# Attention, gated MoE and second MoE on one core: the head reordered, a third point for side work, a pair's last operands split one unit later

## The chip, the cores and the metric

One core of one Trainium2 chip runs the whole program. The metric is device microseconds (us) of one execution; lower is better. Three runs of the kernel before give a median of 1201.41 us (1200.02 to 1201.78).

## The reference

Three stages, everything in float32, with N = 6016 rows and C = 256 channels.

```python
qn = q / (np.linalg.norm(q, axis=1, keepdims=True) + 1e-06)
kn = k / (np.linalg.norm(k, axis=1, keepdims=True) + 1e-06)
s = kn.transpose(0, 2, 1) @ qn / tau               # 256 x 256, over the rows
a = softmax(s)
x = (v @ a).reshape(6016, 256)
...
xn = x / sqrt(mean(x * x, -1) + 1e-06) * rms_g     # gated MoE, d_ff 1536
x = (silu(xn @ w_gate) * (xn @ w_val)) @ w_out
...
h = x @ w_in                                       # second MoE, d_ff 2048
out = (h - np.tanh(h)) @ w_out
```

In the two MoE stages every operand is split into a high and a low part, and every product is made of three matmuls (high·high, low·high, high·low). The weights come as 64-bit words and are put together on the chip. (The first code block is shortened: the softmax stands for four lines.)

## The kernel before

Five engines work under one schedule that the Python program writes out by hand: each engine runs its instructions in the order of the program, so a line that is emitted earlier stands earlier in its engine's queue, and an instruction that waits holds up all behind it on that engine. SP issues nearly all DMAs in the same way. PE is TensorE, DVE VectorE, ACT ScalarE.

**The head.** `attention()` reads q and k in 13 chunks (11 of four 128-row groups, then 2 and 1). For every chunk ACT squares q and k (L463) into `sq`, DVE adds the squares to `acc` (L438), and PE adds the products into S (`score`, L433). The last three chunks (`BEHIND`) leave their products for later. Then PE sums `acc` over partitions into `nrm` (L490), DVE makes the reciprocal norms in a chain of 15 short steps (L501 to L508), PE spreads them (`rq_ps`, L514) between the held-back products, and a loop over the two halves of S does the softmax (L528 to L540). What follows makes x for the first two token blocks (L561), its mean square (L585), its norm (`rsqrt_ops`, `r`, L601) and its split.

**The converter.** Nine weight items (`gv0` to `gv5`, gate and value; `w10` to `w12`, output weights) are converted by the generator `conversion()`: ACT starts the item (`w_start`, L273), DVE shifts it (L277), adds the sign (L280) and the low bits (L284), ACT makes the high part `h`, DVE the low part `l` (L141), and a DMA saves it to DRAM (`gv2s<-gv2y`). The generator yields after each step; `PLAN` gives, for places of the head, how many steps to run there, and `need()` forces an item that a product wants.

**Pair 0.** The first two token blocks (512 and 384 wide) go through 12 `gate_block`s each: gate product, value product, `silu`, multiplication, split, and pushes of output products (`A.push`) into a list of fillers that PE takes `LAG` blocks later. Block 1 runs `SKEW` steps behind block 0. Two calls of `side(a, d)` in every block let the waiting generators (`works`: the converter, the preparation of the next pair's operands `x_work`, the sums of weights) run up to d DVE and a ACT steps; a generator may also wait a number of such calls (`yield 4`). Right behind the head stand `split_a()` and, spread over the first steps, the norm chain of block 1 (`post`).

**Pairs 1 to 5** of the first MoE and **p0 to p5** of the second work on two 512-wide token blocks (448 in p0) in Strassen-like units: seven products per unit (X, T, Y, Z), operands B11, T1, T2, B21, T3, B22, T4 prepared by `operands()` from the pair's four blocks. At a unit's start PE makes X and T, ACT copies them to Y and m5 (L138), PE adds T2's product onto Y, DVE adds Y and m5 to Z (L166). `unit()` calls `hurry()`, which runs the list `urgent`, right behind the two copies. At the end of a pair `finish(x_work)` emits all that is left of the next pair's operands: B21, T3, B22 and T4 may only be split once the last unit of the running pair is under way. The scale of x by its norm (`x_0g<-x_0g,rs`, L769) comes before that; it wants a row that goes by DMA through DRAM (`back<-naryp` L758, then `rs<-back` L763).

## Time and profile before

| | value |
|---|---|
| median of three runs | 1201.41 us |
| the profiled execution | 1201.24 us, its span 1199.3 us |
| mean granted TensorE clock | 0.982 |
| PE busy | 1143.6 us (95%) |
| DVE busy | 826.0 us (69%) |
| ACT busy | 690.9 us (58%) |
| PE on the chain that ended last | 78% of the span (DVE 8%, DMA 6%, ACT 5%) |

The profiled execution took 1.9 us more than its span, which starts with the first instruction recorded. PE is busy nearly all the time, so a gain has to come from a stretch in which PE waits, or runs at the lower of its two clock levels (1.2 GHz, shown as 0.50, and 2.4 GHz, shown as 1.00). The stages follow from the names of the matmuls: the head to 74.83, pair 0 to 188.35, pairs 1 to 5 to 293.85, 401.75, 503.13, 602.99 and 694.69, the six pairs of the second MoE to 773.67, 859.86, 942.24, 1025.08, 1107.46 and the end.

### The profile page before, as it was taken

Reading aid. Unit: us, or ns where it says so; the run is one execution under the profiler, and the core shown is the slowest. Engines: PE = TensorE matmul, PEld = TensorE weight load, DVE = VectorE, ACT = ScalarE, POOL = GpSimd, SP = SyncE. Lnnn points to the kernel's source line nnn. Section 1 sums busy time; section 2 is a strip of 40 time slices with the busy share of each in tenths; the row PEclk is TensorE's granted clock in tenths of the full one; section 3 lists DMA queues with packets and bytes.
Section 4 is the critical chain, followed back from the end, with each engine's and each line's share of the span. In section 5 each row is a group of like instructions: output and inputs, shape, how many; then the busy total and the mean of one; then the engine's idle time right before and its main releaser. Section 6 shows DMA issues by size and latency. Waiting matters only on the chain.

```text
span 1199.3 us, 13912 instructions
## 1 busy us (share of the span) xinstructions
PE 1143.6 (95%) x4980; PEld 931.9 (78%) x4980; DVE 826.0 (69%) x1382; ACT 690.9 (58%) x1207; POOL 0.7 (0%) x6
## 2 busy tenths in 40 slices
PE   9689899998999999999999999899999999999998
PEld 8567597786787777778878888788888788888887
DVE  5677576757657666857777787776776776766664
ACT  5454536554655654564565565665665755756655
POOL 0000000000000000000000000000000000000000
PEclk9798999998999999999999999999999999999999
DMA  9535211211311212031020130010110100100000
GB/s 363 202 110 189 71 53 49 71 34 55 107 43 45 88 62 71 27 106 33 29 93 21 34 104 19 18 58 1 36 36 1 62 10 1 62 1 1 36 1 36
DMA packets 37736, 73.04 MB, mean 61 GB/s; under 512 B 6426, under 2 KB 8218, under 8 KB 37668
## 3 DMA queue, kind: packets, MB, share of 16 engines
q1 hardware_dynamic: 37380, 71.12, 18.0%
q10 hardware_dynamic: 288, 1.05, 0.2%
q8 instruction: 39, 0.64, 0.2%
q14 instruction: 29, 0.24, 0.1%
HBM read 52.45 MB, written 19.70 MB: 60 GB/s over the span
## 4 chain that ended last, share of the span: by engine, by line
PE 78%; DVE 8%; DMA 6%; ACT 5%; issue 2%; SPq 0%; ACTq 0%; DVEq 0%
PE acc L147 32%; PE Yh L147 8%; PE Yg L147 5%; PE Yv L147 5%; PE Xh L147 5%; PE Xv L147 3%; PE Xg L147 3%; PE Zh L147 3%; PE Th L147 2%; PE x L147 2%; DMA k<-k_in 2%; PE g L147 2%; PE v L147 2%; PE Zv L147 2%; PE Tv L147 2%
## 5 line engine op out<-in xcount | busy, mean ns | idle before, releaser
L135 ACT ACTIVATE hc<-wc 128x512 fp32r<-128x512 f32 (+1 forms) x192 | 113.8, 617 | 76.9 <-DVE wc L1188 76.9
L141 DVE TENSOR_TENSOR lc<-wc,hc 128x512 fp32r<-128x512 f32 (+1 forms) x192 | 127.3, 674 | 33.1 <-ACT hc L135 33.1
L135 ACT ACTIVATE uc<-t 128x512 fp32r<-128x512 f32 x120 | 72.1, 627 | 87.5 <-DVE t L844 87.4
L141 DVE TENSOR_TENSOR ulc<-t,uc 128x512 fp32r<-128x512 f32 x120 | 79.7, 685 | 10.1 <-ACT uc L135 7.4
L166 DVE TENSOR_TENSOR Zv<-Yv,m5v 128x512 f32<-128x512 f32 x30 | 21.0, 699 | 77.6 <-ACT x_1g L689 43.8
L166 DVE TENSOR_TENSOR Zh<-Yh,m5h 128x512 f32<-128x512 f32 (+1 forms) x48 | 33.0, 687 | 45.6 <-PE Yh L147 41.5
L1188 DVE TENSOR_TENSOR wc<-Yh,wc 128x512 f32<-128x512 f32 (+1 forms) x48 | 32.7, 680 | 28.5 <-ACT wc L1185 28.5
L1185 ACT ACTIVATE wc<-Xh 128x512 f32<-128x512 f32 (+1 forms) x48 | 28.3, 589 | 38.2 <-PE Xh L147 38.2
L166 DVE TENSOR_TENSOR s<-Yh,m5h 128x512 f32<-128x512 f32 (+1 forms) x48 | 32.6, 679 | 24.5 <-PE Yh L147 24.3
L1185 ACT ACTIVATE wc<-Yh 128x512 f32<-128x512 f32 (+1 forms) x48 | 28.3, 589 | 35.9 <-PE Yh L147 35.9
L166 DVE TENSOR_TENSOR Zg<-Yg,m5g 128x512 f32<-128x512 f32 x30 | 21.0, 699 | 35.1 <-PE Yg L147 32.8
L433 PE MATMUL S<-q,k 128*128 128x256 f32 x188 | 44.1, 398 | 1.0 <-DMA k<-k_in 1.0
L1185 ACT ACTIVATE wc<-s 128x512 f32<-128x512 f32 (+1 forms) x48 | 29.9, 623 | 25.1 <-DVE s L166 25.0
L433 PEld LDWEIGHTS S<-q,k 128*128 128x128 f32 x188 | 37.2, 200 | 7.2 <-DMA k<-k_in 1.3
L1188 DVE TENSOR_TENSOR wc<-s,wc 128x512 f32<-128x512 f32 (+1 forms) x48 | 32.7, 681 | 9.4 <-ACT wc L1185 9.4
L438 DVE TENSOR_TENSOR acc<-acc,sq 128x1024 f32<-128x1024 f32 (+1 forms) x24 | 24.0, 1023 | 18.0 <-ACT sq L463 17.6
L147 PE MATMUL Yh<-T2h,l2s 128*128 128x512 f32 (+1 forms) x96 | 30.5, 399 | 4.9 <-ACT Yh L138 4.2
L847 ACT ACTIVATE t<-Zg 128x512 f32<-128x512 f32 x30 | 17.9, 596 | 28.4 <-PE Zg L147 28.4
L166 DVE TENSOR_TENSOR c<-Yv,m5v 128x512 f32<-128x512 f32 x30 | 20.7, 691 | 18.9 <-PE Yv L147 17.3
L1188 DVE TENSOR_TENSOR wc<-Xh,wc 128x512 f32<-128x512 f32 (+1 forms) x48 | 32.6, 679 | 0.9 <-ACT wc L1185 0.5
L1188 DVE TENSOR_TENSOR wc<-Zh,wc 128x512 f32<-128x512 f32 (+1 forms) x48 | 32.3, 672 | 0.0
L147 PE MATMUL Th<-T1h,l2s 128*128 128x512 f32 (+1 forms) x96 | 29.8, 389 | 2.5 <-ACT l2s L135 1.3
(918 smaller groups left out, 3516.3 us busy)
## 6 DMA issues: line engine op xcount, KB each, us to landing
q<-q_in SPq DMA_DIRECT2D x11, 512.0 KB, 9.5
vraw<-vT_in SPq DMA_DIRECT2D x11, 512.0 KB, 3.9
y<-r SPq DMA_DIRECT2D x22, 256.0 KB, 2.0
y<-y SPq DMA_DIRECT2D x20, 256.0 KB, 3.6
outT<-r SPq DMA_DIRECT2D x20, 256.0 KB, 2.1
...
```

Source lines behind the costliest of these rows:

```text
L135: nc.scalar.activation(out=dst, in_=src, func=AF.Copy, scale=scale)
L141: nc.vector.tensor_sub(out=dst, in0=src, in1=f32(hi))
L147: nc.tensor.matmul(out, a, b, start=start and i == 0, stop=i == 2, skip_group_check=True)
L166: nc.vector.tensor_add(out=o, in0=a, in1=b)
L433: nc.tensor.matmul(S[m][:, :C], kt[:, j, m * P:(m + 1) * P], qt[:, j, :], start=(i == 0 and j == 0), stop=(i == NCH - 1 and j == chunks[i] ...
L438: nc.vector.tensor_add(out=out, in0=a, in1=b)
L847: nc.scalar.activation(out=o, in_=a, func=AF.Silu)
L1185: nc.scalar.activation(out=t[c][:, :n], in_=src, func=AF.Tanh)
L1188: nc.vector.tensor_sub(out=t[c][:, :n], in0=src, in1=t[c][:, :n])
```

## The change

The head is written in a new order. All products of the last three chunks with the first half of S stand ahead of `nrm`, those with the second half right behind it, and `rq_ps` after all of them. The squares go through three buffers in turn. `PLAN` puts fewer conversion steps among the squares: none of gv1 before them all are made. The softmax makes both exponentials first and then both divisions. Block 1's norm chain is emitted ahead of the gate blocks, `split_a` moves into the preparation of pair 1.

Every conversion step is now one of DVE or one of ACT, and a generator runs only steps of one engine in one call of `side`. A gate block has three such calls (a new one between `silu` and the multiplication), the first three steps have a thin table of their own (`EARLY`), block 1 runs two steps behind instead of three, and the output products three blocks behind instead of two.

`finish_late` stops the next pair's preparation before B22 and T4 and leaves these two to `urgent`, so that they are emitted inside the next pair's first unit, behind the copies of X and T. It is used at the ends of pairs 1 to 5 and of p0 to p4: ten times; pair 0 keeps `finish`.

```diff
 PLAN = {
-    ("s", 5): 1, ("s", 6): 1, ("s", 7): 1, ("s", 8): 1, ("s", 9): 1, ("c", 0): 1, ("c", 1): 1,
-    ("c", 2): 1, ("c", 3): 1, ("c", 4): 1, ("c", 6): 1,
+    ("s", 4): 1, ("s", 5): 1, ("s", 6): 1, ("s", 7): 1, ("s", 12): 2, ("c", 1): 3, ("c", 2): 1,
+    ("c", 3): 2, ("f", 0): 1, ("f", 1): 0,
 }
-SIDES = (((1, 1), (1, 2)), ((1, 1), (1, 2)))
+EARLY = (((0, 1), (0, 0), (0, 0)), ((0, 1), (0, 0), (0, 0)), ((1, 1), (0, 1), (0, 0)))
+SIDES = (((1, 2), (1, 2), (1, 1)), ((1, 2), (1, 2), (1, 1)))
...
     def can(self, kind):
-        return self.kind == kind and (kind == "A" or self.acted < Work.clock)
+        return self.kind == kind and self.last[kind] < Work.clock
     def run(self):
-        if self.kind == "A":
-            self.acted = Work.clock
+        if self.kind in self.last:
+            self.last["A" if self.kind == "D" else "D"] = Work.clock
...
     def hurry():
-        for op in urgent:
-            op()
-        urgent.clear()
+        while urgent:
+            urgent.pop(0)()
...
         for i, c in enumerate(items):
             y = c["y"].bitcast(I32)
+            yield "D"
             shift(y)
             yield "D"
-            if before:
-                w_low(before)
-                yield "D"
             sign(y, c["raw"][:, :, 1])
+            yield "D"
+            bits(y, c["raw"][:, :, 0])
+            if "saved" in c:
+                nc.sync.dma_start(out=c["saved"], in_=c["y"])
...
+            yield "A"
+            hi_of(c["h"], c["y"])
+            if i + 2 < len(items):
+                w_load(items[i + 2])
             if i + 1 < len(items):
+                yield "A"
                 w_start(items[i + 1])
             yield "D"
...
+            lo_of(c["l"], c["y"], c["h"])
+            c["ready"] = True
...
-                    pool, tag = ((sp, "sq"), (act, "wraw"))[s]
+                    pool, tag = ((sp, "sq"), (act, "wraw"), (act, "vl"))[(2 * i + s) % 3]
...
+            rest = [(i, j) for i in range(NCH - BEHIND, NCH) for j in range(chunks[i][1])]
+            for i, j in rest:
+                score(i, j, 0)
             for s in range(2):
                 for m in range(KC):
...
-            rest = [(i, j) for i in range(NCH - BEHIND, NCH) for j in range(chunks[i][1])]
             for i, j in rest:
-                score(i, j, 0)
+                score(i, j, 1)
...
+        out["late"] = True
         yield from split(("B22", b22), ("T4", t2))
...
+        if p == 1:
+            yield from split_a()
...
+    for op in p1["rs"]:
+        op()
     at("c", 6)
-    split_a()
...
-    SKEW = 3
-    POST = [6, 5, 9]
-    LAG = 2
+    SKEW = 2
+    LAG = 3
...
         silu(t[:, :n], g[:, :n])
+        side(*sides[2])
         mul(t[:, :n], t[:, :n], v[:, :n])
...
+    def finish_late(w, x):
+        while "late" not in x:
+            w.run()
+            hurry()
+        urgent.append(lambda: finish(w))
...
-        finish(x_work)
+        finish_late(x_work, x_next)
```

How the order moves, at the three places that matter. In names, `sq_0` and `sq_1` are squares of q and k, `gv0y` a weight item at work, `gv0h` its high part.

**The head, ACT**, before: the second half of the squares begins.

```order
L273 ACTIVATE gv0y<-gv0raw 128x1024
L463 ACTIVATE sq_0_255<-q_139 128x1024
L463 ACTIVATE sq_1_258<-k_141 128x1024
L273 ACTIVATE gv1y<-gv1raw 128x1024
L463 ACTIVATE sq_0_276<-q_191 128x1024
L463 ACTIVATE sq_1_279<-k_193 128x1024
L135 ACTIVATE gv0h<-gv0y 128x1024
```

And with the change, at the end of the squares:

```order
L460 ACTIVATE sq_0_330<-q_250 128x1024
L460 ACTIVATE sq_1_335<-k_252 128x1024
L460 ACTIVATE sq_0_340<-q_269 128x512
L460 ACTIVATE sq_1_344<-k_271 128x512
L460 ACTIVATE sq_0_348<-q_288 128x256
L460 ACTIVATE sq_1_351<-k_290 128x256
L138 ACTIVATE gv0h<-gv0y 128x1024
L275 ACTIVATE gv1y<-gv1raw 128x1024
L515 ACTIVATE rq<-rq_ps 128x256
```

The start of gv1, which stood between the squares of two chunks, now stands behind all of them, as does the high part of gv0.

**The head, PE**, from `nrm` to the end of S, before:

```order
L490 MATMUL nrm<-ones,acc 128x2 x4
L433 MATMUL S_109<-q_248,k_250 128x256 x4
L433 MATMUL S_109<-q_269,k_271 128x256 x2
L433 MATMUL S_109<-q_290,k_292 128x256
L433 MATMUL S_110<-q_248,k_250 128x256
L514 MATMUL rq_ps<-ident,r__378 128x128 x2
L433 MATMUL S_110<-q_248,k_250 128x256 x3
L433 MATMUL S_110<-q_269,k_271 128x256 x2
L433 MATMUL S_110<-q_290,k_292 128x256
```

With the change:

```order
L430 MATMUL S_109<-q_250,k_252 128x256 x4
L430 MATMUL S_109<-q_269,k_271 128x256 x2
L430 MATMUL S_109<-q_288,k_290 128x256
L490 MATMUL nrm<-ones,acc 128x2 x4
L430 MATMUL S_110<-q_250,k_252 128x256 x4
L430 MATMUL S_110<-q_269,k_271 128x256 x2
L430 MATMUL S_110<-q_288,k_290 128x256
L511 MATMUL rq_ps<-ident,r__380 128x128 x2
```

The first seven held-back products (S_109 is the first half of S) moved ahead of `nrm`, the other seven between `nrm` and `rq_ps`.

**The end of pair 1, DVE**, where pair 2's operands are made (`x_0g` and `x_1g` are x, `rs` its norm, `t_5` unit 5's tiles), before:

```order
L844 TENSOR_TENSOR t_5_2203<-t_5_2203,Yv_2221 128x512
L844 TENSOR_TENSOR t_5_2174<-t_5_2174,c_5_2247 128x512
L141 TENSOR_TENSOR ulc_2265<-t_5_2203,uc_2262 128x512
L769 TENSOR_TENSOR x_0g<-x_0g,rs_0_2192 128x512
L769 TENSOR_TENSOR x_1g<-x_1g,rs_0_2192 128x512
L769 TENSOR_TENSOR x_0g<-x_0g,rs_1_2194 128x512
L769 TENSOR_TENSOR x_1g<-x_1g,rs_1_2194 128x512
L629 TENSOR_TENSOR t_2274<-x_0g 128x512
L141 TENSOR_TENSOR B11l<-x_0g,B11h 128x512
L629 TENSOR_TENSOR t_2280<-x_1g,t_2274 128x512
```

With the change:

```order
L771 TENSOR_TENSOR x_0g<-x_0g,rs_0_2071 128x512
L169 TENSOR_TENSOR t_5_2189<-Yg_2157,m5g_2159 128x512
L771 TENSOR_TENSOR x_1g<-x_1g,rs_0_2071 128x512
L771 TENSOR_TENSOR x_0g<-x_0g,rs_1_2073 128x512
L771 TENSOR_TENSOR x_1g<-x_1g,rs_1_2073 128x512
L628 TENSOR_TENSOR t_2200<-x_0g 128x512
L279 TENSOR_SCALAR y_2118<-y_2118 128x512
L282 SCALAR_TENSOR_TENSOR y_2118<-raw_2087,y_2118 128x512
L144 TENSOR_TENSOR B11l<-x_0g,B11h 128x512
L628 TENSOR_TENSOR t_2231<-x_1g,t_2200 128x512
L169 TENSOR_TENSOR Zv_2239<-Yv_2225,m5v_2227 128x512
L846 TENSOR_TENSOR t_5_2180<-t_5_2180,Xv_2217 128x512
```

The four products with `rs`, which stood behind everything of unit 5, now stand ahead of its value half (`Zv`, `t_5_2180`), and B11's low part with them.

**The end of p1, ACT** (`hc` is a high part of p1's last unit, `Yh` and `m5h` the copies of the first unit of p2), before:

```order
L135 ACTIVATE hc_7195<-wc_7192 128x512
L135 ACTIVATE hc_7197<-wc_7179 128x512
L135 ACTIVATE B22h<-y_6506 128x512
L135 ACTIVATE T4h<-t_6594 128x512
L138 ACTIVATE Yh_7238<-Xh_7230 128x512
L138 ACTIVATE m5h_7240<-Th_7234 128x512
L135 ACTIVATE hc_7244<-wc_7172 128x512
```

With the change:

```order
L138 ACTIVATE hc_7195<-wc_7192 128x512
L138 ACTIVATE hc_7197<-wc_7179 128x512
L141 ACTIVATE Yh_7230<-Xh_7222 128x512
L141 ACTIVATE m5h_7232<-Th_7226 128x512
L138 ACTIVATE B22h<-y_6498 128x512
L138 ACTIVATE T4h<-t_6625 128x512
L138 ACTIVATE hc_7244<-wc_7172 128x512
```

The two high parts of the late operands moved behind the two copies, so that only the last `hc` follows them. DVE's order stays the same there: the low parts of B21, T3, B22 and T4 stand ahead of the first sum Z of the new unit.

## Rows read from the trace of the kernel before

**Rows 1.** Stages: stretch and length (us), busy time (instructions) by engine, clock, DMA share, GB/s

```profile
0.00:74.83 74.83, 60.39 (x268) 49.87 (x269) 47.13 (x86) 39.38 (x48) 0.70 (x6) 0.91 0.66 248
74.83:188.35 113.52, 101.52 (x436) 82.29 (x436) 78.52 (x135) 53.71 (x90) 0.00 (x0) 0.94 0.32 102
188.35:293.85 105.50, 98.02 (x424) 78.39 (x424) 68.25 (x121) 57.81 (x102) 0.00 (x0) 0.99 0.18 54
293.85:401.75 107.90, 102.35 (x424) 81.11 (x425) 73.87 (x126) 60.20 (x107) 0.00 (x0) 0.95 0.21 61
401.75:503.13 101.38, 98.57 (x426) 78.52 (x425) 69.61 (x120) 58.28 (x104) 0.00 (x0) 1.00 0.21 66
859.86:942.24 82.38, 82.22 (x362) 67.41 (x360) 58.67 (x91) 51.42 (x92) 0.00 (x0) 1.00 0.08 26
```

**Rows 2.** Waits of PE: what waited, for what: us in total, times, longest

```profile
PE nrm L490 <- DVE acc L438: 11.3, 1, 11.3
...
PE Xg L147 <- ACT B11h L135: 4.6, 1, 4.6
PE x L561 <- ACT t L847: 4.2, 1, 4.2
...
PE r L601 <- DVE nary L160: 4.0, 2, 3.7
```

**Rows 3.** Timeline of ACT in the squares: start, us, instruction, idle before and its releaser

```profile
31.12 1.15 ACT L273 ACTIVATE gv1y<-gv1raw 128x1024 f32<-128x1024 f32 x1 [4.98 <-DMA gv1raw<-w_val_in]
```

**Rows 4.** Timeline of DVE in the head

```profile
45.95 1.22 DVE L141 TENSOR_TENSOR gv0l<-gv0y,gv0h 128x1024 fp32r<-128x1024 f32 x1
...
54.13 0.17 DVE L501 TENSOR_SCALAR n__375<-nrm 128x8 f32<-128x8 f32 x1 [0.20 <-PE nrm L490]
...
57.01 0.20 DVE L508 RECIPROCAL r__378<-y__376 128x8 f32<-128x8 f32 x1
...
61.78 1.21 DVE L284 SCALAR_TENSOR_TENSOR gv1y<-gv1raw,gv1y 128x1024 int32<-128x1024 int32 x1
```

**Rows 5.** Timeline of PE in the head

```profile
52.23 1.87 PE L490 MATMUL nrm<-ones,acc 128*128 128x2 f32 x8 [11.33 <-DVE acc L438]
53.96 6.33 PE L433 MATMUL S<-q,k 128*128 128x256 f32 x16
60.12 0.61 PE L514 MATMUL rq_ps<-ident,r__378 128*128 128x128 f32 x4
...
74.83 0.51 PE L147 MATMUL g<-xh,gv0h 128*128 128x512 f32 x1 [0.28 <-ACT xh L135]
```

**Rows 6.** A stretch of the head: length, PE busy (records), granted clock, DMA share, GB/s

```profile
45.70:59.30 13.60, 7.07 (x21) 0.50 0.01 5
```

**Rows 7.** Timeline of ACT in pair 0

```profile
120.58 1.12 ACT L273 ACTIVATE w12y<-w12raw 128x1024 f32<-128x1024 f32 x1 [3.89 <-DMA gv4s<-gv4y]
```

**Rows 8.** Tile `back`: DMA times over its 15 issues (back<-naryp, rs<-back); tile `rs`: first use

```profile
DMA to landing us min/median/max: 1.6/4.0/4.2
...
L769 DVE TENSOR_TENSOR x_0g<-x_0g,rs x10: 681/683/686, 169.0 to 579.2; 128x512 f32<-128x512 f32 x10
```

**Rows 9.** Timeline of PE from the end of pair 1

```profile
293.85 0.80 PE L147 MATMUL Xg<-B11h,gv0h 128*128 128x512 f32 x1 [4.62 <-ACT B11h L135]
...
296.20 0.80 PE L147 MATMUL Xg<-B11l,gv0h 128*128 128x512 f32 x1 [1.13 <-DVE B11l L141]
...
301.10 0.80 PE L147 MATMUL Yg<-T2h,sh 128*128 128x512 f32 x1 [1.50 <-ACT Yg L138]
```

**Rows 10.** Timeline from the end of p0

```profile
776.95 0.61 ACT L135 ACTIVATE B22h<-y 128x512 fp32r<-128x512 f32 x1
...
778.62 0.72 PE L147 MATMUL Yh<-T2h,l2s 128*128 128x512 f32 x2 [2.28 <-ACT Yh L138]
```

**Rows 11.** Timeline from the end of p1

```profile
861.91 0.69 DVE L141 TENSOR_TENSOR B22l<-y,B22h 128x512 fp32r<-128x512 f32 x1
...
862.16 0.72 PE L147 MATMUL Yh<-T2h,l2s 128*128 128x512 f32 x2
...
862.51 0.68 DVE L141 TENSOR_TENSOR T4l<-t,T4h 128x512 fp32r<-128x512 f32 x1
```

More of the change, by code (lines that the diff above doesn't have):

```diff
@@ L43, in __init__ @@
     def __init__(self, steps):
-        self.steps, self.kind, self.ready, self.done, self.acted = steps, None, None, False, -1
+        self.steps, self.kind, self.ready, self.done = steps, None, None, False
+        self.last = dict(A=-1, D=-1, pe=-1)
         self.advance()
@@ L285, in bits @@
             out=y, in0=word, scalar=29, in1=y, op0=ALU.logical_shift_right, op1=ALU.bitwise_or)
-    def w_low(c):
-        lo_of(c["l"], c["y"], c["h"])
-        if "saved" in c:
-            nc.sync.dma_start(out=c["saved"], in_=c["y"])
-        c["ready"] = True
     def conversion():
-        before = None
         yield "D"
@@ L510, in attention @@
             rq_ps = bank("b1", "rq_ps")
-            for x, (i, j) in enumerate(rest):
-                if x == 1:
-                    for m in range(KC):
-                        nc.tensor.matmul(
-                            rq_ps[:, m * P:(m + 1) * P], r_[:, 2 * m:2 * m + 1].to_broadcast([P, P]),
-                            ident, start=True, stop=True)
-                score(i, j, 1)
+            for m in range(KC):
+                nc.tensor.matmul(
+                    rq_ps[:, m * P:(m + 1) * P], r_[:, 2 * m:2 * m + 1].to_broadcast([P, P]),
+                    ident, start=True, stop=True)
             rq = sp.tile([P, C], F32, tag="rq", name="rq")
             nc.scalar.activation(out=rq, in_=rq_ps[:, :C], func=AF.Copy)
+            sm = {}
             for m in range(KC):
@@ L526, in attention @@
                 e_ = ut(f"e{m}")[:, :C]
-                sm = sp.tile([P, 1], F32, tag="sm", bufs=2, name=f"sm{m}")
+                z = sp.tile([P, 1], F32, tag="sm", bufs=2, name=f"sm{m}")
                 nc.vector.tensor_tensor_reduce(
@@ L533, in attention @@
                 nc.scalar.activation(
-                    out=e_, in_=s_, func=AF.Exp, bias=mx, scale=rk, accum_out=sm)
-                if m == 0:
-                    at("c", 1)
-                nc.vector.tensor_scalar_add(out=sm, in0=sm, scalar1=1e-9)
-                nc.vector.reciprocal(out=sm, in_=sm)
-                a_full.append(act_tile("uh", 4, f"a{m}", F32)[:, :C])
-                nc.vector.tensor_scalar_mul(out=a_full[m], in0=e_, scalar1=sm)
+                    out=e_, in_=s_, func=AF.Exp, bias=mx, scale=rk, accum_out=z)
+                sm[m] = z, e_
+            for m, (z, e_) in sm.items():
+                nc.vector.tensor_scalar_add(out=z, in0=z, scalar1=1e-9)
+                nc.vector.reciprocal(out=z, in_=z)
+                a_full.append(cs(f"a{m}")[:, :C])
+                nc.vector.tensor_scalar_mul(out=a_full[m], in0=e_, scalar1=z)
+            at("c", 1)
             nc.scalar.activation(out=mx, in_=ones[:, :1], func=AF.Silu)
@@ L545, in split_a @@
         for m in range(KC):
-            h = wpool.tile([P, C], F32R, tag=f"ah{m}", name=f"ah{m}")
-            l = wpool.tile([P, C], F32R, tag=f"al{m}", name=f"al{m}")
+            h, l = (wpool.tile([P, C], F32R, tag=f"a{x}{m}", name=f"a{x}{m}") for x in "hl")
+            yield "A"
             hi_of(h, a_full[m])
+            yield "D"
             lo_of(l, a_full[m], h)
@@ L994, in attn_moe_kernel, with gate_block @@
         p0["low"](c)
+    for op in p1["rs"]:
+        op()
     at("c", 6)
-    split_a()
     load_v(2)
-    post = p1["rs"] + [p1["spread"]] + [
-        op for c in range(KC)
-        for op in ((lambda c=c: p1["norm"](c)), (lambda c=c: p1["high"](c)), (lambda c=c: p1["low"](c)))]
-    SKEW = 3
-    POST = [6, 5, 9]
-    LAG = 2
+    post = {1: [p1["spread"]] + [
+        lambda c=c, x=x: p1[x](c) for x in ("norm", "high", "low") for c in range(KC)]}
+    SKEW = 2
+    LAG = 3
     A = Accumulate(out1_weight, NF1, [n for _, n in blocks[:2]], to_y(0))
-    def gate_block(b, f, sides, last=False):
+    def gate_block(b, f, sides):
         n = blocks[b][1]
@@ L1021, in gate_block @@
         A.push(b, f, (h[:, :n], l[:, :n]))
-        while len(fillers) > KC * LAG and not last:
+        while len(fillers) > KC * LAG and (b, f) != (1, NF1 - 1):
             fill()
@@ L1047, in attn_moe_kernel @@
         if f < NF1:
-            gate_block(0, f, SIDES[0])
-        for _ in range(POST[min(f, len(POST) - 1)]):
-            if post:
-                post.pop(0)()
+            gate_block(0, f, SIDES[0] if f > SKEW else EARLY[f])
+        for op in post.get(f, []):
+            op()
+        at("f", f)
         if f >= SKEW:
-            gate_block(1, f - SKEW, SIDES[1], f >= NF1 + SKEW - 2)
+            gate_block(1, f - SKEW, SIDES[1])
     force(converter, lambda: converter.done)
@@ L1259, in attn_moe_kernel @@
         if p + 1 < NP:
-            finish(x_work)
+            finish_late(x_work, x_next)
     carry(0)()
```

11 lines of the change are left out of this document (2 added, 9 removed).

## The prediction

> **What bounds the kernel.** I read four views in order: the table by stage, the waits of PE, the timelines around the longest waits, and the granted clock there. The stage table [rows 1] says that PE works nearly without a break in the steady pairs (p2: 82.22 us busy of 82.38), so the only time to win lies in four places. In the head PE sums the squares 11.3 us late [rows 2]. In pair 0 it is idle for 113.52 − 101.52 = 12.0 us and runs at a mean clock of 0.94, which costs up to 0.06 × 113.52 = 6.8 us more. Pairs 1 and 2 are longer than pair 3 by 4.1 and 6.5 us. And at the end of p0 there is a stop of 2.28 us [rows 10]. The waits name the causes: `nrm` for DVE's sums, Xg for B11, x for a late ACT, r for DVE's norm chain [rows 2]. A stop also costs clock: from 45.70 to 59.30, behind the stop that ended at 52.23, PE was granted 0.50 [rows 5, 6], that is the level of 1.2 GHz; pair 2, which begins with the stops of [rows 9], shows a mean of 0.95, pair 3 1.00 [rows 1].
>
> **Head.** Three things leave the path to `nrm`. ACT no longer sits 4.98 us on the load of gv1 in the middle of the squares [rows 3]; it starts gv1 when all squares are made, long after that load. DVE no longer makes the low part of gv0 (1.22 us) in the sum chain [rows 4]; it does so after the softmax. (A shift and a sign step of gv1 go too; I count them as reserve.) So `nrm` comes at 52.23 − 4.98 − 1.22 = 46.0. The first seven held-back products now stand ahead of it, so that PE stops far less long and should keep the upper level. The other seven lie beside DVE's reciprocal chain, which takes 57.01 + 0.20 − 54.13 = 3.1 us [rows 4], and cost nothing while they are no longer than it: sixteen records took 6.33 us at half speed [rows 5], so the fourteen of seven products (two records each) take about 2.8 at full. Then `nrm` at full speed takes about half its 1.87 (0.9), the chain 3.1, and some 0.4 to pass from engine to engine: `rq_ps` at 46.0 + 0.9 + 3.1 + 0.4 = 50.4 instead of 60.12, a gain of 9.7. The softmax loses the bits of gv1 (1.21 us) from between its two halves [rows 4], but its first division now waits for the second exponential, and gv0's low part and three steps of gv1 stand behind it on DVE (four steps, 0.7 to 1.2 us each), in front of the mean square's chain. I take +0.1 together: **−9.8**, the gate blocks begin at 65.0 instead of 74.83. Bounds: −6.5 if DVE's own adds, not ACT, are what ends last (the chain was busy without a gap before 52), −11.5 if the reserve counts in full.
>
> **Pair 0.** All loss is 12.0 idle and at most 6.8 of clock; idle at half speed counts once, so about 18.3, and without any loss the pair would take 95.2. Two of the three long stops have their cause removed: r's 3.71 of its 4.0 us [rows 2] go, because the norm chain of block 1 runs while DVE would be idle ahead of the first gate; x's 4.2 us [rows 2] stood behind `w12y` on ACT, which waited 3.89 us for the save of gv4 [rows 7]; a save is now issued one step earlier, behind the bits. What comes in their place: (a) the conversion of w10 is further behind at the start. Five DVE steps (low part of gv1, shift, sign and bits of w10, its low part; four at 1.22 [rows 4] and a shift of about half that, 5.5 us) have still to run before the first output product, where the order of before had the shift, the sign and gv1's low part behind it in the head. LAG 3 moves that product back by a block, which doesn't cover all of it: 2.1 to 7.3 us, I take 6. (b) Three side points in a block put DVE and ACT steps of conversion between `silu` and the multiplication; a step takes up to 1.22 us [rows 4] and the split waits behind it: 0 to 4, I take 2.9. (c) The preparation of pair 1 waits a number of side calls for its row from DRAM. The write took 1.6, the read behind it 4.0 us [rows 8], 5.6 together. Four calls were two blocks before; three to a block they are one and a third. A block is about 95.2 / 24 = 4.0 us, so 8 us become 5.3, less than 5.6, and DVE stands in front of the product with `rs`. Pair 0 still ends in `finish`, so what is late there falls on the first X. The nearest row is the end of pair 1, where the same chain came last: 4.62 us, then 1.13 and 1.50 [rows 9]. Between 0 and 7.3 I take 3.9. Sum: 95.2 + 6 + 2.9 + 3.9 = 108.0, against 113.52: **−5.5**. Bounds: 97.3 (−16) with (b) and (c) hidden and (a) at 2.1, and 114.5 (+1) with (a) and (b) at their upper ends and (c) a little over 3.9 + clock.
>
> For (c) the Trainium skill has a rule that speaks against shorter waits: "DMA: Bandwidth & Descriptors", section "Rules for kernel authors", wants a DMA issued early and its semaphore waited for late. Its section on the anatomy of one DMA gives a fixed cost of about 2.0 us; the trace has 1.6 for the small write and 4.0 for the read, so by the page alone the pair of transfers would take 4.0 and fit into the 5.3, and (c) would be nothing: 1171.8 in all. The measured times decide.
>
> **Pairs 1 and 2.** The order shows the products with `rs` and B11's split ahead of unit 5's value half instead of behind everything. The 4.62 us stop [rows 9] goes: **−4.6** in pair 1. The stops of 1.13 and 1.50 and the half clock go from pair 2, which then looks like pair 3, whose boundary had none: 107.90 − 101.38 = **−6.5** [rows 1]. Bounds together −11.5 and −7.
>
> **p0 to p1.** Yh waited 2.28 us for its copy, which stood behind B22h (776.95) and T4h, 0.6 us each [rows 10]. Both now stand behind the copies: −1.2, and part of the half clock (the Y product itself then waits for the chain of late low parts): **−1.5**, from −3.5 to +0.5.
>
> **The other eight late ends.** There the Yh copy came just in time at 862.16 [rows 11]. It now comes 1.2 us earlier, a gain of 0.3 at most. But B22h and T4h come about 1.1 us later, their low parts on DVE, 0.60 apart [rows 11], stand ahead of Z and wait for them, and Z's sum must be done before Y's next product, some 2.6 us behind the first. I take +0.3 each: **+2.4**, from −1 to +5.
>
> **Sum.** −9.8 − 5.5 − 11.1 − 1.5 + 2.4 = −25.5, from the profiled execution's 1201.24: 1175.7. That execution lies 0.2 under the median of the runs, which makes no difference here.
>
> **Rivals.** *R1, conversion keeps pair 0.* DVE is busy 78.52 of 113.52 us there [rows 1], and steps taken out of the head come back in it. If they do so in full, pair 0 gains nothing and the head only its lower bound: 1201.24 − 6.5 + 0 − 11.1 − 1.5 + 2.4 = 1184.5. For it: DVE's work only moved. Against: two of the named stops go. *R2, pair 0 nearly at PE's own time.* The three points spread conversion well enough that only the start is late: 97 instead of 108, so 1164.7. For it: the sum of DVE's work fits; against: w10 is later than before. *R3, slower: the late split turns into a stop.* At each of the ten late ends DVE waits for B22h and T4h, Z waits behind their low parts, and Y's product behind Z. From the chain it is short by some tenths; if Z comes 2.4 us late instead, PE stops, and the half clock that follows a stop (as in pair 2) adds about 1.7: 4.1 × 10 = 41 against −26.4 of the other terms: 1215.8. It decides the sign above 2.6 us a boundary. For it: DVE's order is unchanged while what it waits for moved back; against: two products and two fillers of PE lie between. *R4, the change nets to nothing*: the order shows that it does what it says, so only compensation is left.
>
> **Chances.** Forecast 0.58, R1 0.19, R2 0.17, R3 0.04, R4 0.02. A difference within 0.2% (2.4 us) is what a measurement of this kernel can't tell from none. Faster 0.94, same 0.02, slower 0.04. The forecast's own bounds are pair 0's and the head's: 1161 to 1190. Range 1161 to 1190: it holds R1 and R2 and leaves out R3, R4 and what lies beyond R1 and R2.
>
> **What would show it.** Right: `nrm` near 46, no half clock before the softmax, the first gate near 65; no wait of r in pair 0; no stop at Xg at the start of pair 2 and pair 2 near 101.4; no wait of Yh at the start of p1. Wrong: `nrm` still waiting past 49 for DVE; waits of acc for w10 over 7 us or of Xg at the start of pair 1 over 5; any stop of Yh or Zh over 1 us at the starts of pairs 3 to p5.

## The result and the profile after

The changed kernel takes 1185.08 us (median of four runs, 1182.36 to 1186.4) against 1200.72 of before: a ratio of 0.9866 with a 95% interval of 0.9846 to 0.9886, some 16 us faster. Forecast were 1175.7 and a range of 1161 to 1190. The execution that was profiled is the fastest of the four, 1182.36 us with a span of 1180.6; the sums below are made in it, and the 2.7 us to the median are taken up with the head.

The table by stage of the changed kernel, columns as in [rows 1]: the head, pairs 0 to 3, p1 and p2. All but p1 stand against a line there.

```profile
0.00:64.96 64.96, 57.13 (x269) 47.16 (x269) 44.38 (x83) 37.70 (x47) 0.70 (x6) 1.00 0.76 290
64.96:168.81 103.85, 96.41 (x436) 78.91 (x436) 79.00 (x135) 52.21 (x89) 0.00 (x0) 0.98 0.33 105
168.81:271.69 102.88, 99.37 (x425) 79.84 (x425) 70.34 (x125) 58.62 (x105) 0.00 (x0) 0.98 0.17 52
271.69:379.20 107.51, 99.40 (x425) 78.46 (x424) 72.91 (x125) 60.23 (x107) 0.00 (x0) 1.00 0.23 69
379.20:483.29 104.09, 99.86 (x426) 79.92 (x424) 69.83 (x120) 58.82 (x104) 0.00 (x0) 0.98 0.20 64
...
753.72:838.83 85.11, 82.25 (x361) 67.28 (x360) 60.89 (x95) 52.59 (x95) 0.00 (x0) 1.00 0.08 27
838.83:922.06 83.23, 82.19 (x362) 67.44 (x360) 58.79 (x91) 51.40 (x92) 0.00 (x0) 1.00 0.08 26
```

Head −9.9, pair 0 −9.7, pair 1 −2.6, pair 2 −0.4, pair 3 +2.7, p1 −1.1, p2 +0.8. DVE's busy time hardly changed (79.00 against 78.52 us in pair 0): the work is the same and stands elsewhere. The largest miss is visible at once: pair 2 did not become like pair 3.

The head on PE:

```profile
46.14 1.05 PE L490 MATMUL nrm<-ones,acc 128*128 128x2 f32 x8 [1.67 <-DVE acc L435]
47.05 3.27 PE L430 MATMUL S<-q,k 128*128 128x256 f32 x14
50.46 0.68 PE L511 MATMUL rq_ps<-ident,r__380 128*128 128x128 f32 x4
53.84 4.34 PE L560 MATMUL x<-vraw,a 128*128 128x512 f32 x10 [2.69 <-DVE sm L534]
```

Against [rows 5]: `nrm` waits 1.67 instead of 11.33 us and comes at 46.14; the seven products behind it take 3.27 us beside DVE's chain; `rq_ps` starts at 50.46. New is a stop of 2.69 us for the softmax, which products of S used to fill.

PE's waits in pair 0 of the changed kernel, columns as in [rows 2]:

```profile
PE ms L717 <- ACT sh L138: 2.5, 1, 2.5
PE acc L150 <- DVE w10l L144: 1.8, 1, 1.8
PE acc L150 <- ACT w10h L138: 1.3, 1, 1.3
PE v L150 <- DVE t L846: 0.7, 1, 0.7
```

The waits of r and of x [rows 2] are gone. In their place stands the late w10, 1.8 + 1.3 us; the longest stop is now that at `ms` (the mean square of pair 1's x), 2.5 us where it was 1.4 before. All stops together are 103.85 − 96.41 = 7.4 us instead of 12.0. Of DVE's own waits at the end of the pair one is the forecast wait for the row from DRAM:

```profile
159.59 0.69 DVE L771 TENSOR_TENSOR x_0g<-x_0g,rs 128x512 f32<-128x512 f32 x1 [3.17 <-DMA rs<-back]
```

And pair 2, on PE, with the steps of ACT that matter in it:

```profile
273.95 0.50 PE L150 MATMUL Tg<-T1l,sh 128*128 128x512 f32 x1 [0.96 <-DVE T1l L144]
...
276.30 0.51 PE L150 MATMUL Yg<-T2h,sh 128*128 128x512 f32 x1 [1.14 <-ACT Yg L141]
...
279.26 0.50 PE L150 MATMUL Yg<-T3h,gv0h 128*128 128x512 f32 x1 [0.62 <-DVE Zg L169]
...
288.65 0.50 PE L150 MATMUL Tv<-T1h,sh 128*128 128x512 f32 x1 [1.89 <-ACT x_0g L689]
```

```profile
275.13 0.63 ACT L138 ACTIVATE T3h<-x_0g 128x512 fp32r<-128x512 f32 x1 [2.05 <-DVE x_0g L628]
...
285.41 0.66 ACT L1095 ACTIVATE y<-raw 128x512 f32<-128x512 f32 x1 [3.14 <-DMA raw<-w_in_in]
...
349.15 0.66 ACT L1095 ACTIVATE y<-raw 128x512 f32<-128x512 f32 x1 [4.33 <-DMA raw<-w_in_in]
```

The stop of 4.62 us at Xg [rows 9] is gone, but four smaller ones follow. For the second, the copy Yg stood on ACT behind T3h, which waited 2.05 us for DVE. For the last one ACT stood 3.14 us on a load of the second MoE's weights (`y<-raw`), and the copy of x that frees the bank T was queued behind it. A second such wait, 4.33 us at 349.15, is followed by a stop of PE of 1.32 us at 350.86; that one was there before too (1.45).

The clock's part of the forecast for pair 2 did come: it went from 0.95 to 1.00, and PE's busy time from 102.35 to 99.40 us. But its stops within the pair grew from 107.90 − 102.35 = 5.5 to 107.51 − 99.40 = 8.1 us (the 4.62 us lie ahead of the pair's first product and count to pair 1).

### The profile page after: what moved, and what is told of

Its sections match the earlier page's. It is cut to its first block, busy times and chain, and to the rows that moved or that the text cites. A ratio compares the mean times of both kernels' runs of the same rounds, so it can differ in the third digit from the quotient of the medians.

```text
span 1180.6 us, 13927 instructions
## 1 busy us (share of the span) xinstructions
PE 1132.7 (96%) x4980; PEld 925.4 (78%) x4980; DVE 825.0 (70%) x1382; ACT 689.8 (58%) x1207; POOL 0.7 (0%) x6
## 3 DMA queue, kind: packets, MB, share of 16 engines
q1 hardware_dynamic: 37380, 71.12, 18.1%
## 4 chain that ended last, share of the span: by engine, by line
PE 74%; DVE 12%; DMA 5%; ACT 5%; issue 2%; SPq 0%; ACTq 0%; DVEq 0%
PE acc L150 31%; PE Yh L150 8%; PE Xh L150 5%; PE Yv L150 5%; PE Yg L150 4%; PE Xv L150 3%; PE Zh L150 3%; PE Th L150 3%; PE Xg L150 2%; DMA k<-k_in 2%; PE Tv L150 2%; PE x L150 2%; PE Zv L150 2%; PE Tg L150 1%; PE Zg L150 1%
## 5 line engine op out<-in xcount | busy, mean ns | idle before, releaser
L138 ACT ACTIVATE uc<-t 128x512 fp32r<-128x512 f32 x120 | 72.2, 627 | 95.2 <-DVE t L846 95.2
L144 DVE TENSOR_TENSOR ulc<-t,uc 128x512 fp32r<-128x512 f32 x120 | 79.8, 685 | 9.5 <-ACT uc L138 6.9
L430 PE MATMUL S<-q,k 128*128 128x256 f32 x188 | 41.4, 381 | 1.7 <-DMA k<-k_in 1.7
```

The source lines that it names most:

```text
L138: nc.scalar.activation(out=dst, in_=src, func=AF.Copy, scale=scale)
L144: nc.vector.tensor_sub(out=dst, in0=src, in1=f32(hi))
L430: nc.tensor.matmul(S[m][:, :C], kt[:, j, m * P:(m + 1) * P], qt[:, j, :], start=(i == 0 and j == 0), stop=(i == NCH - 1 and j == chunks[i] ...
```

## The experiments

Twelve runs. Each kernel was run beside the kernel before on the same chip; lengths of stages come from one profiled execution each and vary by a us or two with the granted clock. All stages, worked out from where the stages begin on PE (us):

| kernel | head | pair 0 | 1 | 2 | 3 | 4 | 5 | p0 | p1 | p2 | p3 | p4 | p5 |
|---|---|---|---|---|---|---|---|---|---|---|---|---|---|
| before | 74.8 | 113.5 | 105.5 | 107.9 | 101.4 | 99.9 | 91.7 | 79.0 | 86.2 | 82.4 | 82.8 | 82.4 | 91.8 |
| b_late | 75.3 | 113.5 | 105.7 | 106.2 | 101.7 | 100.0 | 91.7 | 79.0 | 84.9 | 83.0 | 83.0 | 83.1 | 92.0 |
| changed | 65.0 | 103.9 | 102.9 | 107.5 | 104.1 | 100.6 | 90.7 | 79.1 | 85.1 | 83.2 | 83.2 | 83.3 | 92.0 |
| a_finish | 65.9 | 105.4 | 102.7 | 108.1 | 102.4 | 100.6 | 90.9 | 79.0 | 86.7 | 82.9 | 83.2 | 83.0 | 91.8 |
| a_can | 66.2 | 104.0 | 106.5 | 106.4 | 102.4 | 99.9 | 91.7 | 79.0 | 84.9 | 83.1 | 83.1 | 83.1 | 92.0 |
| a_two | 68.8 | 127.4 | 114.1 | 111.7 | 107.3 | 111.4 | 95.0 | 79.7 | 85.5 | 83.3 | 83.9 | 83.2 | 91.0 |
| a_pace | 65.9 | 118.1 | 108.5 | 106.9 | 102.0 | 105.0 | 90.7 | 79.1 | 85.2 | 83.2 | 83.8 | 83.2 | 92.1 |
| a_third | 65.5 | 121.9 | 111.8 | 107.5 | 102.3 | 105.1 | 90.7 | 79.0 | 85.1 | 83.2 | 83.7 | 83.2 | 92.0 |
| a_nrm | 70.2 | 104.0 | 103.1 | 107.4 | 102.3 | 100.6 | 90.7 | 79.0 | 85.1 | 83.2 | 83.7 | 83.2 | 92.1 |
| a_warm | 67.0 | 105.7 | 103.1 | 107.4 | 104.2 | 100.6 | 90.7 | 79.0 | 85.1 | 83.2 | 83.2 | 83.4 | 92.0 |
| a_raw | 67.6 | 105.4 | 102.9 | 105.6 | 102.1 | 103.2 | 90.7 | 79.1 | 85.1 | 83.2 | 83.4 | 83.2 | 92.0 |
| a_w2late | 66.5 | 105.5 | 102.7 | 102.1 | 102.0 | 102.7 | 101.5 | 100.5 | 85.6 | 83.2 | 83.7 | 83.2 | 92.1 |
| a_raw2 | 65.7 | 105.5 | 101.5 | 104.1 | 102.0 | 100.6 | 90.7 | 79.8 | 85.1 | 83.2 | 84.0 | 83.2 | 92.0 |
| a_best | 66.9 | 105.2 | 101.9 | 103.8 | 101.7 | 100.6 | 90.7 | 79.0 | 85.1 | 82.9 | 83.3 | 82.9 | 91.8 |

### The late split: put in alone, and taken out

b_late is the kernel before with `finish_late` at the ten ends (and `hurry` popping one at a time).

```diff
-        finish(x_work)
+        finish_late(x_work, x_next)
```

> The kernel before with finish_late alone at the ten ends. Theory: p1 shrinks by 1 to 2 us, p2 to p5 grow by 0.85 each, pair 2 gains about 1, pairs 3 to 5 lose some tenths: no difference of the whole, between -2 and +3 us against the kernel before. Rival (a gain at each end): 3 us or more faster. By my forecast's terms alone it would be +0.9 (-1.5 and +2.4).

Measured: 1202.14 us, ratio 1.0000 (0.9991 to 1.0010). No difference, and the stages show why: pair 2 −1.7 and p1 −1.3 against p2 +0.7, p3 +0.2, p4 +0.7, p5 +0.2, the head +0.5 and some tenths in pairs 1, 3 and 4. Three of its rows (p1, p2 and p4):

```profile
773.12:858.01 84.89, 82.28 (x362) 67.25 (x360) 61.00 (x95) 52.19 (x94) 0.00 (x0) 1.00 0.08 27
858.01:941.04 83.03, 82.20 (x361) 67.41 (x360) 58.79 (x91) 51.56 (x92) 0.00 (x0) 1.00 0.08 26
...
1024.08:1107.15 83.07, 82.23 (x362) 67.41 (x360) 58.82 (x91) 51.56 (x92) 0.00 (x0) 1.00 0.07 23
```

a_finish is the changed kernel with `finish` back at all ten ends.

> The changed kernel with the old finish at all ten ends, so that B22 and T4 are split at once again and their high parts stand ahead of the copies on ACT. Theory (the late split costs about 0.85 us at each end of p1 to p4, where the pairs p2, p3, p4 grew from 82.38, 82.84, 82.38 to 83.2, some tenths at pairs 2 to 4, and gains only where the copies stood in a long queue, pairs 1 and p0): p2 to p5 fall back by 3 us together, pair 2 and p1 grow by 1 to 2 each, the whole between -2 and +1 us against the changed kernel (1183 to 1186). Rival (the late split is a gain at each end, and the growth of the pairs has another cause): p2 to p5 stay at 83.2 or grow, the whole is 3 to 8 us slower (1188 to 1193).

Measured: 1183.39 us (1182.33 to 1187.05), ratio 0.9847 (0.9828 to 0.9865), which overlaps the changed kernel's. p1 grows by 1.6, pair 2 by 0.6, and p2 to p5 lose 0.4, 0.0, 0.2 and 0.3: 0.9 us together, less than the theory's 3 us, with the signs it gave. No worth of the third part of the change can be measured as a whole; the gain of 16 us lies in the other two. What it takes back is seen in p2 of the changed kernel: PE, which did not stop there before, stops 0.35 us at 844.10, where Y's product waits for Zh, and 0.69 us at 852.57 for the copy Yh of the second unit.

### The generators' rule

a_can lets a generator run a step of ACT again in the call in which it ran one of DVE, from pair 1 on.

```diff
-        return self.kind == kind and self.last[kind] < Work.clock
+        return self.kind == kind and (not Work.strict or self.last[kind] < Work.clock)
...
+    Work.strict = False
     w2_work = Work(second_weights())
```

> The changed kernel with the old rule of the generators from pair 1's start on: a generator may again run an ACT step in the call of side in which it ran a DVE step. Pair 0 keeps the new rule. Theory (the new rule makes x_work reach its ACT steps a call later, and that is what moved x's copies in front of Y's copy in unit 4 of pair 3, 1.78 us of wait and half clock, and kept pair 2's T1 and T2 late): pair 3 returns from 104.1 to about 101.5, pair 4 from 100.6 to 99.9, pair 2 falls by 1 to 2; 3 to 6 us faster than the changed kernel (1179 to 1182). Rival (the rule is not it, the late split shifts these): pairs 3 and 4 stay within 0.5, the whole within 1.5 us.

Measured: 1186.33 us, ratio 0.9866 (0.9847 to 0.9885). The theory falls: pairs 2, 3 and 4 return 1.1, 1.7 and 0.8 us, the signs it gave, but pair 1 grows by 3.6 and pair 5 by 1.0, and the 3 to 6 us did not come. Pair 3 came out at 101.7 to 102.4 in most of the other kernels too, without any change of the rule (but at 104.2 in a_warm). Against before, its 104.1 us are 1.3 us more of busy time at a clock of 0.98 (0.98 in a_warm too) and 1.4 us more of stops, the longest 1.78 us at 453.51.

### The pacing of pair 0

a_two puts pair 0's two side points (from the first step on, without `EARLY`), three steps of skew and two of lag back, and keeps the new rule.

```diff
-SIDES = (((1, 2), (1, 2), (1, 1)), ((1, 2), (1, 2), (1, 1)))
+SIDES = (((1, 1), (1, 2)), ((1, 1), (1, 2)))
...
-    SKEW = 2
-    LAG = 3
+    SKEW = 3
+    LAG = 2
...
-        side(*sides[2])
...
```

> The changed kernel with pair 0's pacing of before: two side points in a gate block from the first step on, block 1 three steps behind, output products two blocks behind; the head, the conversion's new steps and all else as changed. Theory (the third point and the longer lag carry the gain of pair 0, the conversion bounds it): pair 0 goes from 103.9 back to 111 to 116, the whole 7 to 12 us slower than the changed kernel. Rival (the gain of pair 0 came with the norm chain of block 1, the earlier saves and the finer steps): pair 0 stays at 102 to 107, the whole within 3 us.

Measured: 1242.34 us, ratio 1.0331 (1.0315 to 1.0347). Far more than either side expected, and not all of it is pair 0 (+23.5): pairs 1 to 5 grew by 33.7 together. I had overlooked that LAG also sets how many output products are left in the list when pair 0 ends. With two blocks of lag and only the last block held back it is a block fewer, and all later pairs run with that shorter reserve; pairs 1 to 4 now have waits of acc for a late low part (`ulc`) of 1.9 to 2.2 us near their start, which the changed kernel does not have. The test was confounded and was mended.

a_pace is a_two with before's two last blocks held back and, in pair 0, before's rule: its pacing in full.

```diff
-        while len(fillers) > KC * LAG and (b, f) != (1, NF1 - 1):
+        while len(fillers) > KC * LAG and not last:
...
-            gate_block(1, f - SKEW, SIDES[1])
+            gate_block(1, f - SKEW, SIDES[1], f >= NF1 + SKEW - 2)
```

> The changed kernel with pair 0's pacing of before in full: two side points a block, block 1 three steps behind, output products two blocks behind with before's two last blocks held back (so that as many output products are left over for the next pairs as in the changed kernel, which a_two had not kept), and the old rule of the generators during pair 0. Head, finer conversion steps, earlier saves and the norm chain ahead of the blocks stay as changed. Theory (the new pacing carries the gain of pair 0, and half of a_two's loss was the missing reserve of output products): pair 0 111 to 116 instead of 103.9, pairs 1 to 5 within 3 us of the changed kernel in sum; the whole 7 to 14 us slower. Rival (the gain came with the norm chain and the saves): pair 0 at 102 to 107.

Measured: 1202.98 us, ratio 1.0005 (0.9995 to 1.0016): the whole gain of the change is gone, although the head still ends at 65.9. Pair 0 takes 118.1 us, above the 111 to 116 expected, and pairs 1 to 5 grow by 7.3 together (pair 1 by 5.6, pair 4 by 4.4), which were to stay within 3:

```profile
65.91:183.97 118.06, 103.17 (x437) 83.93 (x437) 76.22 (x129) 52.33 (x87) 0.00 (x0) 0.91 0.29 94
```

```profile
PE acc L151 <- ACT w11h L139: 4.1, 1, 4.1
PE acc L151 <- DVE w10l L145: 3.7, 1, 3.7
PE Yfirst L1073 <- ACT B11h L139: 2.5, 1, 2.5
PE ms L718 <- ACT sh L139: 1.4, 1, 1.4
```

Of the 14.2 us that pair 0 grows, 7.5 are stops (14.9 against 7.4) and 6.8 busy time at the lower clock (0.91 against 0.98). What the head takes out of the squares comes back in pair 0 as late weights (w10, w11), unless pair 0 runs the conversion faster. The two parts belong together: the shorter head without the new pacing is worth nothing. Which of the points, the rule, the skew and the lag does it, a_pace can't tell, since it changes all of them; of the first a_third tells.

a_third leaves out only the call of `side` behind `silu`.

```diff
         silu(t[:, :n], g[:, :n])
-        side(*sides[2])
         mul(t[:, :n], t[:, :n], v[:, :n])
```

> The changed kernel without the third side point alone; the rule, the early table, two steps of skew and three of lag stay. Theory (with one engine's step a call, two points give the conversion too few steps, so that weights come late by force): stops of acc or g on late weights as in a_two and a_pace, pair 0 at 112 to 122 instead of 103.9 to 105.5, the whole 8 to 18 us slower; the reserve of output products is kept, so pairs 1 to 5 change by under 5. By my forecast's term (b) the third point cost 2.9 us: it would then be up to 3 us faster.

Measured: 1211.75 us, ratio 1.0077 (1.0058 to 1.0096). Expected were 8 to 18 us more than the changed kernel; it is 26.7. Pair 0 takes 121.9, with the weights late and the first operand of pair 1 later still, and pairs 1 to 5 grow by 11.7 together instead of under 5:

```profile
PE Yfirst L1072 <- ACT B11h L138: 11.0, 1, 11.0
PE acc L150 <- ACT w10h L138: 2.8, 1, 2.8
PE acc L150 <- DVE w11l L144: 2.6, 1, 2.6
```

Under a rule of one engine's steps a call, the number of calls is the speed of the side work: of the conversion and, in the longest stop, of the preparation of pair 1. Without the third point the change makes the kernel some 0.8% slower than before. Skew and lag were not taken back one by one, so their share stays open.

### The order of the products around the norms

a_nrm puts `nrm` ahead of all held-back products again and `rq_ps` between those of the second half.

> The changed kernel with before's order of the products around the norms: nrm first, then the seven held-back products with the first half of S, one with the second half, rq_ps, the other six. Conversion steps and square buffers stay as changed. Theory (keeping PE at work up to the norms saves the clock): PE stops from 41 to 46, the clock falls to 0.50 behind nrm, nrm still comes at 46, rq_ps 1 to 3 us later, the head ends at 67 to 69 instead of 65. Rival (the order of the products doesn't matter, only nrm's time does): the head ends within 1 us of 65.

Measured: 1186.46 us, ratio 0.9873 (0.9857 to 0.9889). The head ends at 70.2, with `nrm` at 46.60:

```profile
46.60 1.43 PE L488 MATMUL nrm<-ones,acc 128*128 128x2 f32 x8 [4.13 <-DVE acc L435]
47.89 6.69 PE L430 MATMUL S<-q,k 128*128 128x256 f32 x16
54.41 0.61 PE L511 MATMUL rq_ps<-ident,r__373 128*128 128x128 f32 x4
```

PE stops 4.13 us instead of 1.67, and the products behind the stop take 6.69 us for sixteen records, as in [rows 5], instead of 3.27 for fourteen. Against the heads of the kernels with the new order (65.0 to 68.8, most of them under 67) that is 1.3 to 5.2 us, more than the 2 to 4 expected against the changed kernel. Each head is that of one execution; the interval of the whole overlaps the changed kernel's.

a_warm puts eight products of ones by ones on PE in the stop for the softmax.

```diff
+WARM2 = 8
...
+            for _ in range(WARM2):
+                nc.tensor.matmul(nrm[:, :P], ones, ones, start=True, stop=True)
             rq = sp.tile([P, C], F32, tag="rq", name="rq")
```

> The changed kernel with eight more products of ones by ones, whose result nobody reads, on PE between rq_ps and the first x product, where PE stops for the softmax (from about 51 to 53.8). Theory (this stop is what makes the executions of the changed kernel differ: the granted clock behind it was 1.00 in its profiled execution but 0.70 to 0.92 from 56 to 62 in five others, and their heads ended 1 to 2.7 us later): the head ends at 65 whatever the execution, the median falls by 1 to 2.5 us to 1182.5 to 1184, and the spread of the runs shrinks. Rival (the stop costs nothing in most runs, the differences come from later stops): the median stays within 0.7 of 1185, the head varies as before.

Measured: 1185.81 us (1182.6 to 1187.13), ratio 0.9861 (0.9840 to 0.9882): a miss. The head took 67.0 us and the runs spread as before. The clock from 50 to 62, in the changed kernel, in a_finish, in a_raw and in a_warm, one line each:

```profile
50.00:62.00 12.00, 9.16 (x38) 1.00 0.20 59
```

```profile
50.00:62.00 12.00, 9.31 (x34) 0.86 0.26 81
```

```profile
50.00:62.00 12.00, 9.20 (x26) 0.72 0.24 68
```

```profile
50.00:62.00 12.00, 11.10 (x54) 0.89 0.03 12
```

With the same head, the same program of PE is granted 1.00 in one execution and 0.72 in another. What the clock costs is seen in the ten products of x behind the stop: 4.34, 6.04 and 7.38 us at 1.00, 0.86 and 0.72. The 0.89 of a_warm is a mean of two stretches:

```profile
50.00:56.00 6.00, 5.10 (x28) 0.78 0.01 3
56.00:62.00 6.00, 6.00 (x27) 1.00 0.05 21
```

In that execution the clock fell earlier, behind `nrm`, where the fourteen products took 4.96 us instead of 3.27; behind the filler it was 1.00, and the products of x took 4.35. But a_third, which has no filler, was granted 1.00 from 50 to 62 as well. One execution thus neither shows that the filler holds the clock nor that it doesn't; shown is that the whole gains nothing from it. The heads of the kernels that share this head ended between 65.0 and 67.6, that of a_two at 68.8; besides the clock, `nrm` itself began between 45.3 and 47.1 in them. What decides the clock was not found.

### What keeps pairs 1 and 2

a_raw moves the first ACT step on a piece of the second MoE's weights two calls of `side` further behind its load.

```diff
                     in_=src.rearrange("(k p) f -> p k f", p=P))
-                yield 2
+                yield 4
```

> The changed kernel with one number changed: the conversion of the second MoE's weights waits four calls of side instead of two between the load of a raw piece and its first ACT step, so that this step stands in ACT's queue later than the load lands. Theory (what is left in pairs 1 and 2 is ACT standing 18.1 us in all on these loads, in nine waits, with the copies of x and of Y behind them): the stop of Tv at the start of pair 2 (1.89) and some of the Yg stops go, pair 2 falls by 2 to 4 us, pair 3 by 1 to 2, the whole 3 to 6 us faster than the changed kernel. Rival (PE is held by other work of pair 2 anyway): the ACT waits go and pair 2 stays within 1 us.

Measured: 1185.16 us, ratio 0.9862 (0.9844 to 0.9880). The 3 to 6 us expected did not come. Pair 2 falls by 1.9 (the stop at Tv is gone) and pair 3 by 2.0 (to where it stands in most kernels), and pair 4 grows by 2.5, with a new stop of 2.12 us at 558.44. ACT's waits for the loads moved but did not shrink: 18.7 us in six places against 18.1 in nine. The single buffer is the reason to be tried next: the load is only issued when DVE has done with the piece before it.

a_w2late moves the whole conversion of these weights to pair 3 and later.

```diff
-        yield lambda: sums_work.done
+        yield lambda: sums_work.done and place[0] >= 3
```

> The changed kernel with the whole conversion of the second MoE's weights moved out of pairs 1 and 2: it begins with pair 3. Theory (pair 2 is longer than pair 4 by 6.9 because this conversion shares ACT and DVE with the late operands): pair 2 falls from 107.5 to 101 to 103, pair 1 by 0 to 2; pairs 4 and 5 and p0 grow, so that the whole is not faster. Rival (pair 2 is long because its own operands and those of pair 3 come late, behind the weight sums of pair 1): pair 2 stays above 105.

Measured: 1208.05 us, ratio 1.0054 (1.0034 to 1.0074), as expected no gain (23 us more than the changed kernel), but its pair 2 is what it was made for:

```profile
274.72:376.81 102.09, 98.64 (x425) 78.60 (x424) 63.99 (x109) 56.85 (x101) 0.00 (x0) 1.00 0.11 32
...
581.55:683.01 101.46, 94.86 (x397) 75.65 (x396) 66.49 (x111) 52.27 (x92) 0.00 (x0) 0.97 0.23 72
683.01:783.50 100.49, 85.27 (x362) 73.05 (x361) 70.36 (x136) 55.16 (x108) 0.00 (x0) 0.92 0.15 50
```

102.09 instead of 107.51, with three of the four stops at its start still there (0.96, 1.14 and 0.62). The conversion is what makes pair 2 long; late, it costs pair 5 and p0 32 us.

a_raw2 gives the pieces two buffers, so that each is loaded a whole piece ahead.

```diff
+            raw = (act if x == 0 else late[0]).tile(
+                [P, 2 * C, 2], I32, tag=("wraw", "wraw2")[x], bufs=1, name=f"raw{j}{x}")
...
+                raw = following
+                if (j, x) != (NU2 - 1, 1):
+                    following = load2(j + x, 1 - x)
                 yield 2
```

> The changed kernel with two raw buffers for the second MoE's weights: each piece is loaded one whole piece ahead, so that ACT no longer meets a load that is still under way (18.1 us of ACT waits in nine places; in a_raw, where the step was only moved two calls back, 18.7 remained in six places). Ones and the identity move into the conversion's memory to make room. Theory (these waits hold up the copies of x and Y behind them and make the stops of PE in pairs 1 to 4): ACT's waits on raw are gone, pair 2 falls by 2 to 4 us, pairs 3 and 4 by 1 to 2 each, the whole 4 to 8 us faster than the changed kernel (1177 to 1181). Rival (the work itself, on ACT and DVE, not its waits, makes pair 2 long): waits gone, pair 2 still above 106, the whole within 2 us.

Measured: 1180.06 us (1176.33 to 1181.55), ratio 0.9812 (0.9790 to 0.9835), some 5 us faster than the changed kernel in the medians. Pair 2 falls by 3.4, pair 3 by 2.1 (to where it stands in most kernels), pair 1 by 1.3 (pair 4 nothing). In pair 2 PE's stops fall from 8.1 to 4.8 us: those of 1.89 at Tv and of 1.32 at 350.86, the two behind ACT's waits for a load, are gone. ACT's waits for raw are gone, but more than half of that time (10.8 of 18.1 us) has become another wait, for the save of the piece before, which has one buffer as well:

```profile
  DMA l<-y: 10.8, 4
```

a_best is a_raw2 with the late split kept at the ends of pair 1 and p0 alone.

> a_raw2 (two raw buffers) with the late split kept only at the two ends where the stages showed a gain from it, those of pair 1 and p0; the eight others go back to the old finish. Theory (the late split costs 0.2 to 0.7 us at each of the eight, by the stages of b_late against before: pairs 3, 4 and p2 to p5 +2.1 together): pairs 3 to 5 and p2 to p5 lose 1.5 to 2.5 us against a_raw2's, the median 1177.5 to 1179.5 against its 1180.1. Rival (these tenths are lost in other waits): within 0.7 of a_raw2.

Measured: 1178.98 us (1177.46 to 1179.58), ratio 0.9813 (0.9798 to 0.9829), the same ratio as a_raw2. The stages p2 to p5 fell by 0.4, 0.7, 0.4 and 0.3 as expected, pairs 3 to 5 by 0.3 together. Of a_raw2 and a_best it can't be said which is faster; both beat both kernels.

## Why the prediction was right, and where it was off

The sign and the range held, of the three large terms the head came as forecast, pair 0 gave more and pairs 1 and 2 far less; the sum of −25.5 was too large, since −18.9 was measured in the profiled execution and −16 in the medians. The median lies next to R1's 1184.5, but by chance: R1 let pair 0 gain nothing, and it gained 9.7.

**Head, −9.8: right.** Measured −9.87, and by its steps: `nrm` at 46.14 (46.0 forecast), `rq_ps` at 50.46 (50.4), first gate at 64.96 (65.0). That it fits to a tenth is partly luck: the profiled execution has the shortest head of all with the new order; the others end 0.5 to 2.7 us later, a_two's 3.9. That keeping PE at work matters is supported by a_nrm, in one execution. The claim that PE "should keep the upper level" held up to `rq_ps` in nine of the eleven executions with the new order (the fourteen products took 3.27 us there, 4.82 in a_third and 4.96 in a_warm). Behind the stop of 2.69 us for the softmax, which the forecast does not name, the clock from 50 to 62 was 0.72 to 0.86 in eight of them.

**Pair 0, −5.5: two causes right, the sizes off.** Measured −9.67. Term (a), w10 late, came as 3.0 us of stops instead of 6. Term (c) came as described, DVE 3.17 us in front of the product with `rs`, but was worth less than 3.9: from there DVE ran without a gap, and what PE waited for at the end stood behind it, 0.43 us at Xg (for a copy of ACT) and 1.83 at Tg (for a multiplication of DVE, in pair 1). The Trainium skill ("DMA: Bandwidth & Descriptors", the section on the anatomy of one DMA) gives about 2.0 us of fixed cost; it gives them for DMAs that GpSimd issues, and SP issues these. By an estimate from that figure the two transfers would have fitted and (c) been nothing. The trace shows the write issued at 154.04, the read at 155.59 and DVE going on at 159.59, 5.55 us where 5.6 were forecast, so the measured rows were the better guide:

```profile
154.04 0.36 SPq L760 DMA_DIRECT2D back<-naryp  x1
155.59 0.80 SPq L765 DMA_DIRECT2D rs<-back  x2
```

Term (b) booked the third point as a cost alone, 2.9 us; PE shows 0.73 us of it, a stop for a multiplication, and a_third shows that without the point pair 0 is 16 to 18 us longer. The forecast saw what a step costs where it stands and not that steps run by count of calls. The 95.2 us "without any loss" put the smaller stops at nothing without a reason; that at `ms` is 2.5 us.

**Pairs 1 and 2, −11.1: the step that failed.** "The stops of 1.13 and 1.50 and the half clock go from pair 2, which then looks like pair 3": measured −0.39 instead of −6.5, and −2.62 instead of −4.6 in pair 1. The 4.62 us stop did go, and so did the half clock. But T1's low part and the copy behind T3h still came late (0.96 and 1.14 us of stops), and behind them the pair met the conversion of the second MoE's weights: ACT's 3.14 us on a load became Tv's 1.89. In the kernel before, a load of the same conversion was part of the long stop itself:

```profile
290.64 0.66 ACT L1086 ACTIVATE y<-raw 128x512 f32<-128x512 f32 x1 [4.09 <-DMA raw<-w_in_in]
...
291.84 0.69 DVE L141 TENSOR_TENSOR ulc<-t,uc 128x512 fp32r<-128x512 f32 x1 [1.96 <-ACT uc L135]
```

ACT stood 4.09 us on it, and DVE waited 1.96 us for the `uc` behind it before it came to the products with `rs`. The forecast read that stop as a matter of DVE's order alone; the new order took the stop away and left the load, which now holds up ACT inside pair 2. a_w2late shows that this conversion holds 5.4 us of pair 2, a_raw2 that 3.4 of them come from its loads. Pair 1 also begins with the stop of 1.83 us that term (c) had put on pair 0. Pair 3 carries the same conversion with less: its stops add up to 4.2 us against pair 2's 8.1, since those of pair 2's start are missing but for 0.43, and one alone, of 1.78 us, stands behind a load.

**p0 to p1, −1.5, and eight late ends, +2.4: right, as far as the late split goes.** −1.1 in p1: Yh's wait fell from 2.28 to 1.24 us and did not vanish, as "no wait of Yh" had it. The stages behind the eight other ends (pairs 3 to 5, p0, p2 to p5) grew by 4.9 in the changed kernel, 2.3 of it in p2 to p5 and 2.7 in pair 3, of which 1.0 is there without the late split too (a_finish). In b_late, where the late split stands alone, p1 fell by 1.3 and these eight grew by 2.2. R3 did not occur: in the first unit behind a late split no stop of Yh was over 1.3 us, and only p1's 1.24 was over the 1 us that the forecast had named as a sign of being wrong. What the late split gives at two ends (3.0 us in b_late) it takes back at the others.

In sum the pairs 1 and 2 fell short by 8.1 us, pair 0 gave 4.2 more than forecast, and pairs 3 to 5, where only tenths were forecast, lost 2.4: 2.7 in pair 3, half of it clock and half stops.
